# Two loads moved behind the crossbar transposes of chunk 1 in a fused attention and gated-MLP kernel

## The chip, the cores and the metric

The kernel runs on one core of a Trainium2 chip. The time is device microseconds (us) of one execution, as the median of several. Each execution also reports its span, the part that the profile covers (about 2.2 us shorter), and its mean granted TensorE clock, where 1.0 is full speed. All executions told here were classed as fast (at most 1.5% above the fastest of the same kernel measured with them), except the single one of the third run of before, whose state is unknown because it stands alone.

## The reference

```python
x  = A_x                               # 1 x 2048 x 640, bf16
xn = layernorm(x)
out = x + A(xn, wqkv, wo) + B(xn, w_gate, w_up, w_down)

def A(x, wqkv, wo):    # 32 heads of 20, sliding window of 256, causal
    q, k, v = split(x @ wqkv)
    p = softmax(where(mask, q @ k.T * 20**-0.5, -1e9))
    return (p @ v) @ wo

def B(x, w_gate, w_up, w_down):        # 640 -> 1536 -> 640
    return (sigmoid(x @ w_gate) * (x @ w_up)) @ w_down
```

## The kernel before

The 2048 rows are worked in four chunks of 512. TensorE is kept busy by a list called fill: while ScalarE computes the exponentials of one chunk's attention, TensorE gets pieces of other work from that list (gate and up products, the Q, K and V projections of the next chunk, output projections), in an order fixed when the program is built. Chunk 1's normalised rows (`xn`) are transposed into `xnT` by four crossbar DMAs, one per 128 rows, which are emitted inside fill's first part. Nearly all DMAs are issued by SyncE, in program order.

```python
    def load_x(c):
        t = xp.tile([P, SBC, D], BF16, name="xc")
        xc[c] = t
        nc.sync.dma_start(out=t, in_=xr[:, c * SBC:(c + 1) * SBC, :])

    def load_rest():                        # emitted after chunk 0's Q/K projections
        for k in range(1, F // FS):
            load_gu(k)                      # second half of the gate and up weights
        clear("q", 1)
        clear("k", 1)
        nc.sync.dma_start(out=wd, in_=B_w_down.rearrange("(c p) d -> p c d", p=P))
        wo_i = tc.dram_tile([HG, NG * DH, D], BF16, name="wo_i")
        for i in range(HG):                 # shuffle the rows of Wo, DRAM to DRAM
            nc.sync.dma_start(out=wo_i[i].rearrange("(g d) n -> g d n", d=DH),
                              in_=A_wo.rearrange("(g i d) n -> i g d n", i=HG, d=DH)[i])
        for i in range(HG):                 # each load waits for its wo_i[i]
            nc.sync.dma_start(out=wo[32 * i:32 * i + 32, :, :],
                              in_=wo_i[i].rearrange("(m j) n -> j m n", j=32))
        load_x(2)
    # ... cut ...
    def turn_block(c, s):                   # the crossbar transpose
        nc.sync.dma_start(out=xnT[c][:, :, s * P:(s + 1) * P], in_=xns.pop((c, s)), transpose=True)
    # ... cut ...
    fill.add("gu0", mix(g_gu(0, 0, 12), g_norms(1, True), 9), 12 * GU)   # holds the four turns of chunk 1
    fill.add("qk1", g_qk(1), 50 * MM)                                    # first reader of xnT of chunk 1
    fill.add("v1", g_v(1), 40 * 136)
```

The softmax here doesn't subtract the row's maximum and nothing guards it: scores larger than these inputs give would overflow.

## Time and profile before

| | |
|---|---|
| three timed executions (a fourth, 334.03 us, ran later beside the changed kernel) | 333.55, 333.68, 334.47 us |
| the execution that was profiled | 330.59 us, span 328.4, mean clock 1.000 |
| TensorE busy / idle in that profile | 313.5 / 14.9 us |

What binds the kernel is shown in the prediction. Here is the same place in the chain of work that ended last (start, length, what), as the profile followed it:

```profile
58.36 3.77 DMA xnT<-xn
62.12 0.14 issue
62.26 0.39 PE pqk L257
```

The chain goes through the last of the four transposes: from its issue at 58.36 to its landing at 62.12, and then into the first Q/K projection. Across this stretch nothing but that DMA sets the end. TensorE's wait for it, from 58.92 to 62.26 us, is called the hole below.

### The profile page before, as it was taken

The numbers are of one execution on the slowest core, as the hardware profiler recorded it, in microseconds if no ns is written. First come the engines' busy times: TensorE is split into PE (matmuls) and PEld (weight loads), VectorE is DVE, ScalarE is ACT, GpSimd is POOL, SyncE is SP. The second block draws the span as 40 slices with busy tenths as digits, with TensorE's granted clock in tenths as the row PEclk, the third lists the DMA queues.
The fourth block names the chain that finished last, engine by engine and source line by source line (L and its number), as shares of the span: only waits on it lengthen the run. The fifth ranks groups of instructions, "written<-read, shape, count | busy, mean of one in ns | idle before, by whom it ended". The sixth has DMA issues, their size and how long they took to land.

```text
span 328.4 us, 7074 instructions
## 1 busy us (share of the span) xinstructions
PE 313.5 (95%) x2794; PEld 160.6 (49%) x2823; DVE 159.6 (49%) x325; ACT 219.1 (67%) x272; POOL 161.4 (49%) x305
## 2 busy tenths in 40 slices
PE   7999999599999999999999999999999999999996
PEld 2654333245456654544455654544445654444664
DVE  5332476456695443546852363643443425544142
ACT  3824878477867668778866659788786658788200
POOL 3000586256576655455864555665554545555200
PEclk9999999999999999999999999999999999999999
DMA  7976997726400452630014113710000000000001
GB/s 257 373 270 203 370 365 229 90 90 196 128 2 22 100 151 86 191 115 0 3 22 94 28 54 97 243 47 2 2 0 22 23 20 22 0 2 2 0 22 60
DMA packets 34336, 32.86 MB, mean 100 GB/s; under 512 B 9568, under 2 KB 33760, under 8 KB 34272
## 3 DMA queue, kind: packets, MB, share of 16 engines
q1 hardware_dynamic: 33872, 32.01, 31.6%
q8 instruction: 22, 0.36, 0.5%
q10 hardware_dynamic: 432, 0.41, 0.4%
q14 instruction: 10, 0.08, 0.1%
HBM read 21.00 MB, written 10.26 MB: 95 GB/s over the span
## 4 chain that ended last, share of the span: by engine, by line
PE 82%; ACT 6%; DMA 3%; DVE 3%; issue 2%; POOL 1%; SPq 0%; ACTq 0%; DVEq 0%
PE pg L349 15%; PE pu L356 14%; PE pqk L257 13%; PE y L375 12%; PE ps L424 9%; PE acc L450 6%; PE y L388 6%; ACT pT L430 6%; PE pv L284 6%; DMA xnT<-xn 2%; DMA xc<-in_A_x_dram 1%; DVE stats L210 1%; DVE xn L229 1%; DVE t L460 0%; DVE h L360 0%
## 5 line engine op out<-in xcount | busy, mean ns | idle before, releaser
L430 ACT ACTIVATE pT<-ps 128x1024 bf16<-128x1024 f32 (+1 forms) x184 | 175.0, 1004 | 62.9 <-PE ps L424 58.6
L435 POOL TENSOR_SCALAR_AFFINE_SELECT pT<-pT 128x512 bf16<-128x512 bf16 x128 | 82.0, 642 | 89.9 <-ACT pT L430 87.8
L439 POOL TENSOR_SCALAR_AFFINE_SELECT pT<-pT 128x512 bf16<-128x512 bf16 x112 | 71.5, 638 | 54.5 <-ACT pT L430 54.5
L360 DVE SCALAR_TENSOR_TENSOR h<-th,pu 128x512 bf16<-128x512 f32 x48 | 32.7, 682 | 57.1 <-ACT th L352 28.0
L349 PE MATMUL pg<-xnT,wg 128*128 128x512 bf16 x225 | 59.1, 380 | 1.2 <-DVE h L360 0.4
L356 PE MATMUL pu<-xnT,wu 128*128 128x512 bf16 x236 | 58.9, 380 | 0.5 <-issue 0.5
L375 PE MATMUL y<-wd,h 128*128 128x320 bf16 x384 | 56.8, 300 | 0.0
L257 PE MATMUL pqk<-xnT,wqkv 128*128 128x512 bf16 x190 | 45.0, 381 | 4.4 <-DMA xnT<-xn 3.6
L375 PEld LDWEIGHTS <-h 128*128 128x128 bf16 x384 | 35.6, 98 | 18.0 <-issue 5.1
L424 PE MATMUL ps<-qT,kT 20*128 20x384 bf16 (+2 forms) x704 | 39.6, 275 | 2.7 <-ACT pT L430 2.1
L460 DVE STREAM_TRANSPOSE t<-acc 128x512 f32<-128x512 f32 x32 | 22.8, 714 | 33.2 <-PE acc L450 32.9
L356 PEld LDWEIGHTS <-wu 128*128 128x128 bf16 x240 | 22.1, 98 | 27.9 <-issue 3.3
L352 ACT ACTIVATE th<-pg 128x512 f32<-128x512 f32 x48 | 28.8, 601 | 10.1 <-PE pg L349 9.7
L349 PEld LDWEIGHTS <-wg 128*128 128x128 bf16 x240 | 21.3, 98 | 27.7 <-issue 6.5
L257 PEld LDWEIGHTS <-wqkv 128*128 128x128 bf16 x200 | 22.2, 119 | 23.4 <-issue 6.4
L393 DVE SCALAR_TENSOR_TENSOR y_sb<-y,xc 128x320 bf16<-128x320 f32 x32 | 15.4, 491 | 34.4 <-PE y L388 34.3
L424 PEld LDWEIGHTS <-kT 20*128 20x128 bf16 x704 | 11.9, 92 | 33.7 <-issue 33.6
L450 PE MATMUL acc<-pT,v 128*32 128x384 bf16 (+2 forms) x704 | 25.6, 277 | 0.1
L388 PE MATMUL y<-wo,oc 128*128 128x320 bf16 x160 | 24.0, 299 | 0.0
L284 PE MATMUL pv<-wqkv,xnT 128*128 128x320 bf16 x160 | 23.8, 300 | 0.0
L261 DVE CAST st<-pqk 128x512 bf16<-128x512 f32 x20 | 13.7, 691 | 16.0 <-PE pqk L257 16.0
L450 PEld LDWEIGHTS <-v 128*32 128x32 bf16 x704 | 14.6, 96 | 13.6 <-issue 10.2
(36 smaller groups left out, 160.4 us busy)
## 6 DMA issues: line engine op xcount, KB each, us to landing
qT<-sq SPq DMA_DIRECT2D x3, 1024.0 KB, 5.8
kT<-sk SPq DMA_DIRECT2D x3, 1024.0 KB, 5.6
sq<-st SPq DMA_DIRECT2D x20, 128.0 KB, 2.1
sk<-st SPq DMA_DIRECT2D x20, 128.0 KB, 3.9
out_dram<-y_sb SPq DMA_DIRECT2D x15, 160.0 KB, 1.8
wg<-in_B_w_gate_dram SPq DMA_DIRECT2D x2, 960.0 KB, 10.9
wu<-in_B_w_up_dram SPq DMA_DIRECT2D x2, 960.0 KB, 10.9
xc<-in_A_x_dram SPq DMA_DIRECT2D x3, 640.0 KB
```

The source lines that it names most:

```text
L257: nc.tensor.matmul(ps, lhsT=wt[:, m, :], rhs=xnT[c][:, d, :], start=(d == 0), stop=(d == DC - 1))
L284: nc.tensor.matmul(ps[:, 0:HALF], lhsT=xnT[c][:, d, s * P:(s + 1) * P], rhs=wqkv[:, d, 2 * D + hf * HALF:2 * D + (hf + 1) * HALF], start=( ...
L349: nc.tensor.matmul(pg, lhsT=part(wg, d, f), rhs=xnT[c][:, d, :], start=(d == 0), stop=(d == DC - 1))
L356: nc.tensor.matmul(pu, lhsT=part(wu, d, f), rhs=xnT[c][:, d, :], start=(d == 0), stop=(d == DC - 1))
L360: nc.vector.scalar_tensor_tensor(out=h, in0=th, scalar=1.0, in1=pu, op0=ADD, op1=MULT)
L375: nc.tensor.matmul(ys[hf], lhsT=ht[c, f][:, s * P:(s + 1) * P], rhs=wd[:, f, hf * HALF:(hf + 1) * HALF], start=(f == 0), stop=False)
L388: nc.tensor.matmul(ys[hf], lhsT=oc[c, m][:, s * P:(s + 1) * P], rhs=wo[:, m, hf * HALF:(hf + 1) * HALF], start=False, stop=(m == DC - 1))
L424: nc.tensor.matmul(pss[i // 2][:, i % 2, col * P:(col + n) * P], lhsT=qk["k", kc][32 * i:32 * i + DH, g, kb * P:(kb + 1) * P], rhs=qk["q", ...
L430: nc.scalar.activation(out=pt[:, 2 * a:2 * a + 2, 0:width * P], in_=pss[a][:, :, 0:width * P], func=EXP, scale=SCALE)
L435: nc.gpsimd.affine_select(out=v, in_=v, pattern=[[0, HG], [1, P]], compare_op=GE, fill=0.0, base=0, channel_multiplier=-1)
L439: nc.gpsimd.affine_select(out=v, in_=v, pattern=[[0, HG], [-1, P]], compare_op=GE, fill=0.0, base=-1, channel_multiplier=1)
L450: nc.tensor.matmul(acc[32 * i:32 * i + 32, q0 * P:(q0 + n) * P], lhsT=v[:, h * VW:h * VW + 32], rhs=pt[:, i, col * P:(col + n) * P], start ...
```

## The change

It was meant to let SyncE issue the transposes of chunk 1 as soon as their blocks are normalised, by sending two things that are needed later (x of chunk 2 and the four loads of Wo) after them. The DRAM shuffle `wo_i` stays where it was.

```diff
+    wo_i = tc.dram_tile([HG, NG * DH, D], BF16, name="wo_i")
+
     def load_rest():
         ...
         nc.sync.dma_start(out=wd, in_=B_w_down.rearrange("(c p) d -> p c d", p=P))
-        wo_i = tc.dram_tile([HG, NG * DH, D], BF16, name="wo_i")
         for i in range(HG):
             nc.sync.dma_start(out=wo_i[i]. ... )
+
+    def load_wo():
         for i in range(HG):
             nc.sync.dma_start(out=wo[32 * i:32 * i + 32, :, :],
                               in_=wo_i[i].rearrange("(m j) n -> j m n", j=32))
-        load_x(2)
...
-    def later(c):
-        load_x(c)
+    def later(load, *args):
+        load(*args)
         yield 0
...
     fill.add("gu0", mix(g_gu(0, 0, 12), g_norms(1, True), 9), 12 * GU)
+    fill.add("x2", later(load_x, 2), 0)
     fill.add("qk1", g_qk(1), 50 * MM)
     fill.add("v1", g_v(1), 40 * 136)
+    fill.add("wo", later(load_wo), 0)
...
```

More of the change, by code (lines that the diff above doesn't have):

```diff
@@ L559 @@
     fill.add("gu0", mix(g_gu(0, 0, 12), g_norms(1, True), 9), 12 * GU)
+    fill.add("x2", later(load_x, 2), 0)
     fill.add("qk1", g_qk(1), 50 * MM)
     fill.add("v1", g_v(1), 40 * 136)
+    fill.add("wo", later(load_wo), 0)
     fill.add("gu1a", mix(g_gu(1, 0, 3), norms2, 0, 2, False), 3 * GU)
     fill.add("out0", mix(g_out(0), norms2, 0, 3), OUT)
-    fill.add("x3", later(3), 0)
+    fill.add("x3", later(load_x, 3), 0)
     fill.add("qk2", g_qk(2), 50 * MM)
```

## The prediction

> **What bounds the kernel now.** I read the busy shares first, then the 40 slices, then who waited for whom on TensorE, then the hole that this pointed to, and last the DMA-issuing queue of SyncE ahead of that hole.
>
> ```profile
> PE 313.5 (95%) x2794; PEld 160.6 (49%) x2823; DVE 159.6 (49%) x325; ACT 219.1 (67%) x272; POOL 161.4 (49%) x305
> ...
> PE   7999999599999999999999999999999999999996
> ...
> PEclk9999999999999999999999999999999999999999
> DMA  7976997726400452630014113710000000000001
> ```
>
> TensorE is busy 313.5 of 328.4 us at full clock, so 14.9 us of idle is all that any reordering of loads can win. One slice in the middle, the eighth (57.5 to 65.7 us), reads 5. The DMA row is full ahead of it and mostly empty afterwards: the loads are crowded into the start. The waits of TensorE from 60 us to the end, its idle time of a quarter of a microsecond or more by releaser:
>
> ```profile
> PE pqk L257 <- DMA xnT<-xn: 3.6, 2, 3.3
> PE ps L424 <- ACT pT L430: 1.5, 6, 0.5
> PE pqk L257 <- issue: 0.5, 3, 0.2
> ```
>
> The only wait on a DMA is that of the Q/K projections for xnT, the crossbar-transposed normalised x: 3.6 us, of which one wait is 3.3. The timeline of TensorE gives its place:
>
> ```profile
> 57.98 0.67 PE L450 MATMUL acc<-pT,v 128*32 128x384 bf16 x16
> 58.58 0.34 PE L424 MATMUL ps<-qT,kT 20*128 20x384 bf16 x4
> 62.26 1.03 PE L257 MATMUL pqk<-xnT,wqkv 128*128 128x512 bf16 x3 [3.33 <-DMA xnT<-xn]
> ```
>
> TensorE ends its last other work at 58.92 and starts chunk 1's projections at 62.26. The other 0.27 us falls at 118 us, on chunk 2. What SyncE's queue did before that hole:
>
> ```profile
> 34.86 0.59 SPq L179 DMA_DIRECT2D wd<-in_B_w_down_dram  x1
> 35.50 8.07 SPq L182 DMA_DIRECT2D wo_i<-in_A_wo_dram  x4
> 49.62 4.09 SPq L185 DMA_DIRECT2D wo<-wo_i  x4
> 53.77 0.43 SPq L133 DMA_DIRECT2D xc<-in_A_x_dram  x1
> 54.25 5.83 SPq L241 DMA_TRANSPOSE xnT<-xn  x4
> ```
>
> and what it waited for from 43 to 54.2 us:
>
> ```profile
> SPq L185 <- DMA wo_i<-in_A_wo_dram: 8.6, 4, 6.0
> ```
>
> From 43.57 to 53.7 us SyncE stands at the four loads of wo, each waiting for its part of wo_i (the row shuffle of Wo through DRAM) to land. Only then can it issue x of chunk 2 and the four transposes. VectorE had the blocks ready long before:
>
> ```profile
> 42.04 0.45 DVE L229 TENSOR_SCALAR xn<-xc,mv,rstd 128x640 bf16<-128x640 bf16 x1
> 46.16 0.84 DVE L229 TENSOR_SCALAR xn<-xc,mv,rstd 128x640 bf16<-128x640 bf16 x1
> 47.77 0.45 DVE L229 TENSOR_SCALAR xn<-xc,mv,rstd 128x640 bf16<-128x640 bf16 x1 [0.17 <-POOL rstd L224]
> 51.11 0.84 DVE L229 TENSOR_SCALAR xn<-xc,mv,rstd 128x640 bf16<-128x640 bf16 x1 [2.89 <-POOL rstd L224]
> ```
>
> They end at 42.49, 47.00, 48.22 and 51.95 us. So the first transpose waits 11.8 us after its input is there and the last one (issue from 58.36) 6.4 us. This is head-of-line blocking on an in-order queue, and it ends in the one hole of TensorE.
>
> [...] the 8.6 us stand on SyncE's queue, while the DMA engines go on moving 131 to 381 GB/s (half-microsecond windows from 48 to 54 us). [...] wd, issued at 34.86, needed 14.8 us to land, and the parts of wo_i behind it let SyncE go on at 49.6, 50.5, 52.0 and 53.4. [...] two transposes alone at 107 to 110 us moved at most 164 GB/s. [...]
>
> **The change, part by part.**
>
> Removed ahead of the transposes: the four loads of wo with their 8.6 us of waiting and four issues of 0.31 us, and the issue of x2 with 0.43 us: 10.3 us of SyncE's queue, 43.57 to 53.77 plus gaps. Also 4 x 200 KB and 640 KB, 1440 KB of traffic. At the 250 to 300 GB/s of that stretch that is about 5 us of ring time (an estimate), part of which lay before the last transposes.
>
> Moved: with the queue free at 43.57, each transpose goes out when its block is ready. An issue takes 1.21 to 1.72 us, mostly 1.27. So: first 43.6 to 44.9, second 47.0 to 48.3, third 48.3 to 49.6, fourth 52.0 to 53.3. To landing, counted from the start of the issue, the trace shows 2.6 us undisturbed and up to 4.3. For the fourth: 52.0 + 2.6 = 54.6 at the earliest, 52.0 + 4.3 = 56.3 at the latest seen. But it also lies behind wo_i, whose last part landed at 53.4[...]. Behind it come the four transposes' own data, 4 x 160 KB at 160 GB/s = 4 us if none had gone earlier. Bad end: 53.4 + 4.1 = 57.5[...]. TensorE needs it at 58.9. So by both sums the wait goes, with 0.4 to 4 us to spare: 3.33 us gained.
>
> Moved behind: x2 is now issued at once after the fourth transpose, at about 53.4. Its 640 KB take some 2.5 us and are over before the first Q store of chunk 1 (about 61 us). Its reader, the statistics of chunk 2, runs with chunk 1's gate and up products, from 84.5 us in the profile of before. Wo goes out behind the V projections of chunk 1, directly after the load of kT (81.7 us before, 78.4 after the gain). kT's 1024 KB move in about 3.5 us (83 to 86.6 us before), then 800 KB of wo in about 3: landed near 87. Its first reader stood at 98.07, so now near 94.8: 7 us to spare. The scores of chunk 1, which need that kT, begin at 91.5 in before with kT landed at about 87.3; even if wo took half the bandwidth kT would keep its slack of 4 us. So cost on the path: 0.
>
> Given back: the first scores after the hole move from 63.44 to about 60.1 us, but ScalarE's two exponentials of the step before run 59.02 to 60.53 and hold the second score buffer. In before the hole hid that. The like sequence at 77.08 us (four score matmuls, five projections, eight score matmuls) waited 0.21 us for ScalarE and others up to 0.5. I take 0.3. TensorE's instructions and order stay the same, and everything later is paced by TensorE, so the rest moves up as a block.
>
> Sum: -3.33 + 0.3 = -3.0 us. 333.68 - 3.0 = **330.7 us**, 0.9% less. The profiled span should go from 328.4 to about 325.4.
>
> **The rivals.**
>
> (a) The transposes are no longer held by SyncE but by the ring. [...] If the fourth lands at 60 rather than 57, about 1.2 us of the hole stays: saving 1.8, 331.9 us. [...]
>
> (b) A new wait takes its place: x2 ahead of the Q stores, or wo ahead of kT, delays the spread of q and k, and TensorE stops at chunk 1's first scores. [...] Against: slacks of 4 to 7 us. If it came, 1 to 3 us back: 332 to 334 us.
>
> (c) The engines behind TensorE used the hole to catch up; without it ScalarE is the bound for some microseconds (it is 5.00 of 5 busy from 70 to 75 us) and the gain is eaten slowly. Against: ScalarE itself was idle 3.40 us before 63.93 for want of scores, and GpSimd 4.18 us before 66.0, so there was no backlog. If true: saving about 2, 331.7 us.
>
> (d) More than the hole: the 0.27 us at chunk 2 goes too, and the waits after it fall better. 330 us.
>
> **Range and chances.** Full closing without give-back is 330.3; rivals (a) and (c) give 331.7 to 331.9, and the three runs of before spread over 0.9 us. So 329.5 to 332.6 holds it 8 times in 10. For more than 2% the time must fall below 327.1, that is 6.6 us or nearly half of all TensorE idle, and this change touches one wait of 3.3: 3%. Slower than 340.4 would need a new wait of 7 us; the nearest slack that could turn into one is larger than the delay: 3%. Within 2%: 94%.
>
> **What would show it.** Right: the loads of wo gone from SyncE's queue before 54 us; the four transposes issued apart, from about 43.6, the last near 52; the wait of the Q/K projections on xnT down from 3.6 to about 0.3 us; the slice that read 5 at 9; a wait of the scores on the exponentials of a few tenths near 60 us. Wrong: a remainder of more than 1 us at the first projection (rival a: its releaser is still the transpose, with more than 4.3 us to landing); new TensorE waits on qT, kT or wo between 75 and 100 us (b); more waiting of scores on ScalarE by 1 us or more (c). If the last transpose lands by 57 and the time still stays above 332.6, my reading of what TensorE waits for is false.

Cuts in the recorded text are marked; what is cut rested on things that no trace or run of this case shows. The sum is whole: -3.33 + 0.3 = -3.0, so 330.7 us. Two terms of the working behind it are cut. One is 1 us for the completion of the last transpose, an assumption: with it the bad end came to 58.5 us, without it to 57.5, and "0.4 to 4 us to spare" counts with it. (In the profile of before the last data moved at about 61.5 us, and the landing stands at 62.12, 0.6 us later.) The other is a guess of 52 to 53 us for the landing of `wo_i`, which the sum did not use. The "ring" means the transfers issued ahead; that they are served in the order of issue was assumed, not shown. Rival (a) rested on one stretch of the profile of before: from 59.0 to 60.5 us the DMAs moved 7 to 44 GB/s while the fourth transpose had yet to land. Why is not shown.

## The result, and the profile after

The changed kernel took 328.96 us (median of four, 328.0 to 330.01) against 333.86 us for the kernel before. The ratio is 0.9852, with a 95% interval of 0.9816 to 0.9887. All ratios here are the mean time of one kernel's fast runs over that of the other's fast runs of the same rounds, so not quite the ratio of the medians. The gain is 4.9 us where 3.0 was predicted, and 328.96 is below the range of 329.5 to 332.6.

Yet between the two profiles the span shrank only from 328.4 to 326.5 us, by 1.9. So the two profiles alone cannot explain the result. First, what they do show. Busy time of TensorE, its slices and its clock, after the change:

```profile
PE 316.7 (97%) x2823; PEld 161.0 (49%) x2823; DVE 159.9 (49%) x325; ACT 219.1 (67%) x272; POOL 161.0 (49%) x305
...
PE   7999989999999999999999999999999999999995
...
PEclk9999999999999999999999999999999999999999
```

The slice that read 5 reads 9. (Some records of matmuls were missing in the first profile, 2794 against 2823, so the busy sums are not compared.) SyncE's queue, with start, length, issued DMA and count:

```profile
36.58 7.93 SPq L183 DMA_DIRECT2D wo_i<-in_A_wo_dram  x4
44.62 10.54 SPq L243 DMA_TRANSPOSE xnT<-xn  x4
55.20 0.58 SPq L133 DMA_DIRECT2D xc<-in_A_x_dram  x1
...
79.35 0.37 SPq L274 DMA_DIRECT2D kT<-sk  x1
79.78 2.38 SPq L188 DMA_DIRECT2D wo<-wo_i  x4
```

The transposes now go out from 44.62 us on, the first of them 3.1 us ahead of the second, and their issues end at 55.16, 4.9 us earlier than before (60.08). The last lands at 57.05 us (53.95 and 3.1 to landing), 2.7 us before TensorE needs it. The loads of Wo stand behind that of kT, at 79.78. TensorE at the place of the hole:

```profile
59.50 0.34 PE L426 MATMUL ps<-qT,kT 20*128 20x384 bf16 x4
59.77 1.27 PE L259 MATMUL pqk<-xnT,wqkv 128*128 128x512 bf16 x5
60.98 0.34 PE L426 MATMUL ps<-qT,kT 20*128 20x384 bf16 x2
61.50 0.39 PE L426 MATMUL ps<-qT,kT 20*128 20x384 bf16 x6 [0.18 <-ACT pT L432]
61.82 2.35 PE L259 MATMUL pqk<-xnT,wqkv 128*128 128x512 bf16 x10
64.10 0.68 PE L452 MATMUL acc<-pT,v 128*32 128x256 bf16 x16
```

The projection follows the scores at once: the hole is gone. The second group of scores is broken, two matmuls, then a wait for ScalarE, then six: this is the give-back that was predicted. Its size shows against the same stretch of before, which ran without that break:

```profile
63.44 0.40 PE L424 MATMUL ps<-qT,kT 20*128 20x384 bf16 x8
63.77 2.35 PE L257 MATMUL pqk<-xnT,wqkv 128*128 128x512 bf16 x10
66.05 0.67 PE L450 MATMUL acc<-pT,v 128*32 128x256 bf16 x16
```

From the first projection to the accumulation it was 62.26 to 66.05, 3.79 us. It is now 59.77 to 64.10, 4.33 us. So 0.54 us were given back, not 0.3.

This profile also has a wait that the first did not: TensorE stood 1.10 us at 42.5 us for the second half of the up weights. With the hole (3.33), the give-back (0.54) and that wait (1.10), the 1.9 us between the two profiles is nearly accounted for: 3.33 - 0.54 - 1.10 = 1.7. The 3 us between the profile of before and the usual execution of before are not. They are what the experiments had to find.

### The profile page after: what moved, and what is told of

The parts are those of the page before. It is cut to its first block, busy times and chain, and to the rows that moved or that the text cites. A ratio compares the mean times of both kernels' runs of the same rounds, so it can differ in the third digit from the quotient of the medians.

```text
span 326.5 us, 7103 instructions
## 1 busy us (share of the span) xinstructions
PE 316.7 (97%) x2823; PEld 161.0 (49%) x2823; DVE 159.9 (49%) x325; ACT 219.1 (67%) x272; POOL 161.0 (49%) x305
## 4 chain that ended last, share of the span: by engine, by line
PE 79%; ACT 7%; DMA 6%; DVE 3%; issue 2%; SPq 1%; POOL 1%; ACTq 0%
PE pg L351 13%; PE pqk L259 13%; PE pu L358 13%; PE y L377 13%; PE ps L426 8%; PE acc L452 7%; PE y L390 6%; ACT pT L432 6%; PE pv L286 6%; DMA wu<-in_B_w_up_dram 4%; DMA xnT<-xn 1%; DMA xc<-in_A_x_dram 1%; DMA sk<-st 1%; DVE stats L212 1%; DVE xn L231 1%
## 5 line engine op out<-in xcount | busy, mean ns | idle before, releaser
L441 POOL TENSOR_SCALAR_AFFINE_SELECT pT<-pT 128x512 bf16<-128x512 bf16 x112 | 71.6, 639 | 54.6 <-ACT pT L432 54.6
L358 PE MATMUL pu<-xnT,wu 128*128 128x512 bf16 x240 | 59.8, 380 | 1.1 <-DMA wu<-in_B_w_up_dram 1.1
L351 PE MATMUL pg<-xnT,wg 128*128 128x512 bf16 x240 | 59.9, 380 | 0.4 <-DVE h L362 0.4
L259 PE MATMUL pqk<-xnT,wqkv 128*128 128x512 bf16 x200 | 46.5, 382 | 0.3 <-DMA xnT<-xn 0.3
```

The costliest lines, as they stand in the source:

```text
L259: nc.tensor.matmul(ps, lhsT=wt[:, m, :], rhs=xnT[c][:, d, :], start=(d == 0), stop=(d == DC - 1))
L351: nc.tensor.matmul(pg, lhsT=part(wg, d, f), rhs=xnT[c][:, d, :], start=(d == 0), stop=(d == DC - 1))
L358: nc.tensor.matmul(pu, lhsT=part(wu, d, f), rhs=xnT[c][:, d, :], start=(d == 0), stop=(d == DC - 1))
L441: nc.gpsimd.affine_select(out=v, in_=v, pattern=[[0, HG], [-1, P]], compare_op=GE, fill=0.0, base=-1, channel_multiplier=1)
```

## The experiments

Two chips served: the runs of the first and third group were on one, those of the second group on another. The kernel before was run beside every group.

**Group 1: what the usual execution of before looks like, and which half of the change does it.** The first two kernels are before and after, unedited.

> The kernel before, unchanged, to see how its own runs spread. Theory A (the hole in front of chunk 1's Q/K projections is 3.3 us in one profile, but varies; the three timed runs, 333.6 to 334.5, had a larger one than the profiled run, which took 330.59 us): runs scatter between about 330 and 335 us, and a profile of a run near 334 us shows a hole of about 6 us. Theory B (the hole is always 3.3 us and the extra gain of the changed kernel came from elsewhere): a run near 334 us still shows 3.3 us there, and the excess stands at another place.

Measured: 333.93 us (six runs, 332.76 to 335.2), ratio 1.0007 to itself. The profiled execution was a usual one this time, 333.51 us. Its hole was 3.72 us and not 6, and its mean clock was 0.993. Its span is 2.8 us longer than that of the first profile, and 0.4 of this is in the hole (3.72 against 3.33), 0.8 in the start before it (TensorE's last work ends at 59.68, not 58.92) and 1.6 just behind it, in matmuls that ran slow. So theory A missed, and theory B was right only in that the excess stands mostly outside the hole. The third profile below shows the slow matmuls best.

> The changed kernel, unchanged. Theory A: no wait on the transposes at the first projection in any profile; 328 to 330 us; the wait for the second up-weights (1.1 us at 42 us in the first profile) comes and goes and makes most of that spread. Theory B: same time, but the profile of it shows another part shorter than in before.

Measured: 328.96 us (327.67 to 330.51), ratio 0.9858, clock 1.000 in all six executions. No wait for the up weights in this profile. The hole is gone here too.

Only the loads of Wo moved:

```diff
     (the changed kernel, but)
+        load_x(2)          # at the end of load_rest, as before
-    fill.add("x2", later(load_x, 2), 0)
```

> Only the loads of wo are moved behind; x of chunk 2 stays ahead of the transposes, issued at about 44 us. Theory A1 (SyncE's standing at the loads of wo made the hole): nearly the whole gain, 328.5 to 330 us, hole under 0.5 us. Theory A2 (the traffic ahead of the transposes in the ring made it): half of the gain or less, 331 to 332.5 us, with a hole of 2 us or more.

Measured: 328.63 us (327.92 to 329.56), ratio 0.9846: all of the gain. The queue of SyncE in this run:

```profile
45.05 0.45 SPq L133 DMA_DIRECT2D xc<-in_A_x_dram  x1
45.61 11.06 SPq L244 DMA_TRANSPOSE xnT<-xn  x4
```

x of chunk 2 is issued ahead of the transposes, and TensorE still had no wait of a quarter us or more at the first projection. So with SyncE's standing at the loads of Wo gone, x's 640 KB of traffic ahead makes no hole.

Only x of chunk 2 moved:

```diff
     (the changed kernel, but the loads of wo stay in load_rest)
-    def load_wo():
-    fill.add("wo", later(load_wo), 0)
```

> Only x of chunk 2 is moved behind the transposes; the loads of wo stay ahead. Theory A1: SyncE still stands until about 53.4 us; the transposes start 0.5 us earlier and without 640 KB before them: gain of 0.5 to 2 us, 332 to 333.3 us. Theory A2: more than half of the gain, 330 to 331 us.

Measured: 331.53 us (330.19 to 332.51), ratio 0.9932, a gain of some 2.3 us. That lies between the ranges of the two theories. Mean clocks went from 0.990 to 1.000; three of the six executions had 0.999 or more. The hole in its profile, which is that of the fastest of the six executions (330.19 us):

```profile
54.30 5.87 SPq L241 DMA_TRANSPOSE xnT<-xn  x4
...
61.77 1.25 PE L257 MATMUL pqk<-xnT,wqkv 128*128 128x512 bf16 x5 [2.30 <-DMA xnT<-xn]
```

SyncE stands as long as before (transposes from 54.30, against 54.25 in the first profile), yet the hole is 2.30 us: with x's 640 KB issued behind them, at 60.22 us, the wait for the transposes ended at 61.77, not 62.26. That is 1.0 to 1.4 us less than in the three profiles of before; the rest of the 2.3 us fits the better clock that group 2 goes into. So x alone explains a part of the hole, and moving it is worth something only while the loads of Wo hold the transposes back. The two halves do not add up: by the ratios (times the 333.9 us of before) x alone gives 2.3 us, Wo alone 5.1 and both together 4.7, the last two the same within their intervals.

**Group 2: the clock.** One more profile of before, unedited:

> The kernel before once more, for one more profile. Theory clock: the TensorE work after the hole up to the waits at 77 to 80 us is longer than the 14.8 us of the first profile (62.26 to 77.08) by 1.5 us or a multiple wherever the mean clock is under 1, and the hole is 3.3 to 4 us. Theory length: that stretch is 14.8 us and the hole is what grew.

Measured: 333.82 us, mean clock 0.989, hole 3.50 us. TensorE from the hole on:

```profile
62.69 2.30 PE L257 MATMUL pqk<-xnT,wqkv 128*128 128x512 bf16 x5 [3.50 <-DMA xnT<-xn]
64.92 0.61 PE L424 MATMUL ps<-qT,kT 20*128 20x384 bf16 x8
65.47 3.59 PE L257 MATMUL pqk<-xnT,wqkv 128*128 128x512 bf16 x10
68.98 0.68 PE L450 MATMUL acc<-pT,v 128*32 128x256 bf16 x16
```

The same ten projections that took 2.35 us in the first profile take 3.59, and from the first projection to the accumulation it is 62.69 to 68.98, 6.29 us against 3.79. The windows of one microsecond of this run tell why (busy time and instruction count of TensorE, its weight loads, VectorE, ScalarE, GpSimd, then the granted clock, the DMA share and GB/s):

```profile
60.00:61.00 1.00, 0.00 (x0) 0.00 (x0) 0.51 (x2) 0.79 (x2) 0.14 (x1) 1.00 0.37 77
61.00:62.00 1.00, 0.00 (x0) 0.00 (x0) 0.00 (x0) 0.00 (x0) 1.00 (x2) 0.60 1.19 245
62.00:63.00 1.00, 0.31 (x1) 0.16 (x2) 0.00 (x0) 0.00 (x0) 0.08 (x1) 0.50 0.00 0
...
67.00:68.00 1.00, 1.00 (x3) 0.29 (x2) 0.17 (x1) 0.56 (x1) 0.30 (x1) 0.50 0.38 128
68.00:69.00 1.00, 1.00 (x9) 0.37 (x8) 0.52 (x1) 0.00 (x0) 1.00 (x3) 0.99 0.00 0
```

The clock falls to half in the middle of the hole (0.60 as the mean of the window from 61 to 62 us means that it fell at about 61.2) and stays there until 68.0: 6.8 us. It costs 6.29 - 3.79 = 2.5 us of TensorE's path. In the other slow profile of before it was half from about 63.9 to 67.3 us, 3.4 us, and cost 63.40 to 68.76 less 3.79, 1.6 us. In the first profile, on which the prediction rested, it did not fall at all before the end of the program.

The profiles leave no other place for the missing 3 us. From the accumulation behind the ten projections to the end of the span, all thirteen profiles take 262.0 to 262.5 us (before: 328.4 - 66.05, 331.2 - 68.76, 331.4 - 68.98; changed: 326.5 - 64.10, 326.3 - 63.89, 325.9 - 63.44). The start scatters in both kernels: TensorE's last work in front of the hole ends at 58.92, 59.68 and 59.18 us before, at 59.84 (with the wait of 1.10 us), 59.62 and 59.17 after. So the two usual executions profiled in group 1, 4.9 us apart in span, differ by 3.72 for the hole and 1.6 for the clock, less 0.54, and by about 0.1 elsewhere.

Does the clock account for the usual execution? The 30 executions of before in these groups, on both chips, sorted by their mean clock:

| mean clock | executions | mean us |
|---|---|---|
| 1.000 | 2 | 331.25 |
| 0.993 to 0.995 | 11 | 333.08 |
| 0.989 to 0.990 | 9 | 333.96 |
| 0.983 to 0.985 | 8 | 335.02 |

The clocks come in steps of 0.005 to 0.006, which over a span of 331 us is 1.7 to 2.0 us of full-speed time, or 3.3 to 4.0 us at half clock: one, two or three such stretches, by this estimate. (A thousandth or two below 1 is nothing lost: the mean also counts a fall after the last matmul. In the run with 6 matmuls below, the last matmul ends at 325.29 us, the clock falls at about 327.4, and this alone makes its 0.998.) Only two of the 30 kept the full clock, like the execution first profiled (330.59). The slow executions need not differ in the clock alone, so this is a correlation. The next kernel takes the clock away and leaves the hole:

```diff
+    def busy(n):
+        ps = ps_d.tile([P, CW], FP32, name="pbusy", tag="d")
+        for k in range(n):
+            nc.tensor.matmul(ps, lhsT=ident, rhs=wg[0][:, 0, 0:CW], start=(k == 0), stop=(k == n - 1))
+        yield 0
...
+    fill.add("busy", busy(13), 0)
     fill.add("qk1", g_qk(1), 50 * MM)
```

> The kernel before, with 13 matmuls of 128x512 on tiles that are there anyway, results unused, put in front of chunk 1's Q/K projections: 13 x 0.216 = 2.8 us of work inside the hole, which stays as long as it was (the transposes land when they landed). Theory clock [...]: clock 1.0 in all runs, idle at the first projection under 1 us, 330.8 to 331.8 us, that is 2.3 to 3 us under the kernel before. Theory length (the hole was simply longer in the usual run than in the first profile): no change, 333.5 to 334.5 us, or longer by what the matmuls overrun.

The theory of the clock: the granted clock falls to half in or after the hole, as it did in the profile of before in group 1 (0.50 for 3.4 us, at a cost of 1.6 us), and matmuls in the hole would keep it up. The 0.216 us a matmul agrees with the profile: one alone took 0.38 us and the 13 took 2.98, so 0.217 for each further one.

Measured: 331.85 us (330.38 to 332.05), ratio 0.9937 (interval 0.9907 to 0.9966), clock 1.000 in all six executions. Adding 13 useless matmuls, 2.98 us in the profile, made the kernel 2.1 us faster (0.63% of 333.7). In the profile they fill most of the hole, and the transposes still end it about where they did (this profile, too, is that of the fastest of its six executions, 330.38 us, so the hole of the usual one is not shown):

```profile
59.05 2.98 PE L561 MATMUL pbusy<-wg,ident 128*128 128x512 bf16 x13
62.38 1.25 PE L257 MATMUL pqk<-xnT,wqkv 128*128 128x512 bf16 x5 [0.35 <-DMA xnT<-xn]
```

The median is 0.05 us above the upper end of what the theory of the clock expected, and the gain a little under it (1.8 us between the medians, 2.1 by the ratio). The theory of length, which expected no change, falls.

The same with `busy(6)`:

> The same with 6 matmuls, 1.3 us: 2.0 to 2.5 us of the hole stay idle. Theory clock: an idle stretch as in the run with only x of chunk 2 moved (2.3 us), where the clock fell in some runs only: mean clock 0.995 to 1.0 and 331 to 332.5 us. Theory length: no change, 333.5 to 334.5 us.

Measured: 331.86 us (330.86 to 332.86), ratio 0.9951. The profiled execution (330.86 us) had 2.10 us of idle and full clock there; four of the six had a mean clock of 0.994, so one stretch at half clock. The time lies within what the theory of the clock expected (the clock of 0.994 just outside), but it does not order itself below the 13 matmuls by as much as the clocks say: the medians are equal and the mean is 0.3 us higher, where one stretch in four of six runs should cost about 1 us. With 13 matmuls nearly the whole hole is used up, so a part of the difference may be their overrun in executions whose transposes land earlier; no profile shows it.

The last kernel of this group has nothing to do with the prediction. It goes after the wait for the up weights:

```diff
     (the changed kernel, but)
-        for k in range(1, F // FS):
-            load_gu(k)
+        for h0 in (0, FS // 2):
+            for t, w in ((wg, B_w_gate), (wu, B_w_up)):
+                nc.sync.dma_start(out=t[1][:, :, h0:h0 + FS // 2],
+                                  in_=w.rearrange("(c p) f -> p c f", p=P)[:, :, FS + h0:FS + h0 + FS // 2])
```

> The changed kernel with the second half of the gate and up weights loaded in four pieces (gate, up, gate, up, 384 columns each) in place of two, so that the piece needed first, at 40 to 42 us, is there after 960 KB and not after 1920. If the wait for the up weights (1.1 us, 0 and 0.6 us in the three profiles with wo moved) costs its length: 328.0 to 328.8 us, 0.3 to 0.9 us under the changed kernel, and no such wait in the profile. If it is covered later: 328.9 us as the changed kernel.

Measured: 327.54 us (327.2 to 328.21), ratio 0.9817 to the kernel before. It is faster than expected, and its executions lie within 1.0 us where those of the changed kernel in group 1, on the other chip, lie within 2.8.

**Group 3: the cross-check.** The 13 unused matmuls in the changed kernel, which has no hole for them:

> The 13 unused matmuls put at the same place of the changed kernel, which has no hole there. If the kernel before with them kept its hole and lost only its clock penalty, then here they must cost their own length: 328.96 + 2.8 = 331.8 us (331.3 to 332.3), the same as the kernel before with them (331.85 us). If they are free here too, the hole was never worth its length: 329 us.

Measured: 330.07 us (329.73 to 330.91), ratio 0.9892, clock 0.999 to 1.000. They cost 1.8 us over the changed kernel of the same group, so they are not free; but the expected 2.8 missed something that the profile shows: with them the next scores no longer wait for ScalarE, so the give-back of 0.54 us is saved again. That makes 2.3. The remaining 0.5 us are within the scatter of the executions, and I leave them open. The other half of the expectation missed as well: the kernel before with the same 13 matmuls took 331.85 us on the other chip, 1.8 us more and not the same. In the two profiles, from the first useless matmul to the accumulation, it is 7.12 against 6.60 us, so 0.5 of the 1.8 is seen, and 1.3 stays open.

> The changed kernel again, beside the next run on the same chip: 328.5 to 329.3 us, clock 1.0 in every run; wait for the up weights between 0 and 1.5 us in the profile.

Measured: 328.27 us (327.83 to 329.01), ratio 0.9844, clock 0.999 to 1.000 (1.000 "in every run" was a little too strict). No wait for the up weights in the profile.

> The changed kernel with the second half of the gate and up weights in four pieces, again. If the 1.4 us it was faster by are the wait for the up weights and its scatter: 327.2 to 328.0 us with the spread half of that of the changed kernel. If they were chance: 328.5 to 329 us.

Measured: 327.61 us (327.22 to 328.16), ratio 0.9819. On the same chip in the same rounds it is 0.66 us under the changed kernel by the medians. So the gain of the split repeats, and this version beats both kernels. The ranges overlap a little, though, and the spread, expected at half that of the changed kernel, is 0.94 us against 1.18 in these rounds. The list of TensorE's waits has no row on a load of weights; its first two of five rows are:

```profile
PE ps L428 <- ACT pT L434: 2.3, 9, 0.5
PE pt L241 <- DVE xn L233: 1.5, 2, 1.2
```

But the profile of the changed kernel beside it had no wait for the up weights either, so that this wait is what the split saves is not shown. It appeared in three of five profiles of kernels with the loads of Wo moved and the weights in two pieces (1.10, 0.64 and 1.21 us), and in none of the six with the loads of Wo in their old place. All of that work is issued ahead of anything the change moves, so I take it for scatter, but these runs do not settle it.

## Why the prediction was right or wrong

- **What makes the hole** was right. SyncE stood at the loads of Wo; with those alone moved, all of the gain came (328.63 us). The transposes then went out 4.4 to 9.6 us earlier, and the wait of 3.33 us at the first projection went to nothing measurable.
- **The times of issue** were right for the first (44.6 us where 43.6 was said) and late for the rest: issues of 2.99 and 2.85 us, where at most 1.72 was allowed for, put the fourth at 53.95 and not 52.0. What made these two long is not shown: the first of the four, behind the same loads, took 1.31, and the median of all twelve in this profile is 1.26. The first three also took 10.7, 8.2 and 5.7 us from issue to landing, where at most 4.3 had been seen. So being issued early did not bring them in early: they landed at 55.3, 55.9 and 56.5 us, after wd (issued at 35.95, landed at 53.9). The bad end of the prediction's sum had allowed for a late landing. It cost nothing: the fourth landed at 57.05 us, inside the 54.6 to 57.5 that was worked out (58.5 with the term that is cut).
- **The moved loads cost nothing**: right. No profile after the change shows TensorE waiting for Wo, kT or qT.
- **The give-back** was right in its mechanism and undersized: 0.54 us where 0.3 was put in.
- **The step that failed** is the first term of the sum, "-3.33", together with the line that carries it: "333.68 - 3.0". The hole was given the worth of its own length and no more, under "busy 313.5 of 328.4 us at full clock". In the usual executions of before that were profiled the clock fell to half in or after the hole (0.50 for 3.4 and 6.8 us). Filling the hole with matmuls that do nothing, which keeps the clock and not the hole's end, gave 2.1 us by the ratio. Read from the two profiles of the usual kind, the clock costs 1.6 and 2.5 us. The term missing from the sum is therefore about -2.1, and the corrected sum is: the length 3.3 to 3.7 (three profiles: 3.33, 3.50, 3.72), less 0.54, plus 2.1, so 4.9 to 5.3 us, against 4.9 measured at first and 4.7 and 5.2 by the ratios of the two later runs of the changed kernel.
- The statement that "14.9 us of idle is all that any reordering of loads can win" falls for the same reason: busy time at half clock is also to be won. The figure itself was too high: 29 matmul records were missing from that profile, and where all 2823 are there and the clock is full, TensorE is busy 316.5 us (only x moved), which would leave about 12.
- **What could have told it before**: the profiled execution took 330.59 us, and the three timed ones 333.55 to 334.47. The time to be explained was not the one that was profiled, and 3 us of it were in no row that I read. What the clock would do could not be read from that profile, where it stayed at 1.00 through the hole of 3.33 us. Nor does the length of a hole alone tell it in these runs: in one profile of before the clock fell at about 61.2 us, some 2.0 us after TensorE's last work (59.18), in another only at 63.9 us, after work had begun again. With 2.10 us of idle in the profiled execution of the run with 6 matmuls the clock held, yet four of the other five of that kernel had a mean clock of 0.994; how long they were idle is not known.
- **Rivals**: (a), the transfers issued ahead in place of SyncE's queue, fits the long landings (up to 10.7 us), though what held them is not shown, and cost nothing: no wait at the first projection, not even in the run that had x ahead of the transposes. (b), a new wait on a moved load, did not come. (c), ScalarE as the bound, was no more than the give-back. (d), more than the hole, was right in its direction only: it named the wait of 0.27 us at chunk 2, and that stayed (0.28 us in the profile after).
- **One reading of the trace** was too low: transposes on their own at 107 to 110 us moved at most 164 GB/s in a microsecond, but two others, alone in the hole of the third profile of before, moved 245 (the window from 61 to 62 us), and 259 in that of the run with 6 matmuls. The estimate of 4 us for four of them was on the safe side, and nothing hung on it.
- **The range** took its spread from three executions and did not allow for the profile being of an exceptional one; its lower end was half a microsecond too high.

What stays open: how the 2 us of the clock share out exactly (the run with 6 matmuls fits them only roughly), 0.5 and 1.3 us of the cross-check, when the clock falls and when not, and the up weights' wait (the corrected sum leaves it out: 1.10 us in one of three profiles of the changed kernel).

## What to carry to other kernels

Before subtracting a wait from a time, check that the profiled execution is the one whose time you subtract from: compare its time, and the mean clock of every execution, not only the clock row of one page. A hole in TensorE's work can cost more than its length, because the matmuls after it may run at half clock: here holes of 3.50 and 3.72 us cost 2.5 and 1.6 us on top. And on a queue that issues in program order, as SyncE's did here (the first transpose, its input ready at 42.49 us, went out at 54.25, behind a load that had waited for its part of `wo_i` until 53.41), put an issue that must wait for another DMA behind everything that is ready sooner.
